# Six subtractions of a fold moved from VectorE to GpSimd, and five drains behind SyncE's last store

## The chip, the cores and the metric

The kernel runs on one core of a Trainium2 chip. The metric is device time in microseconds (us) of one execution; medians over several executions are quoted, lower is better. TensorE does the matrix products, VectorE and ScalarE the elementwise work, GpSimd small statistics and some DMA issues, SyncE most DMA issues. All runs told here were of the fast state.

## The reference, cut to what matters

```python
xn = layernorm(x)                                   # x: 1 x 2048 x 640, bf16
s  = irfft2(rfft2(xn) * (w_r + 1j * w_i))           # spectral filter
g  = silu((gelu(xn @ w_gate) * (xn @ w_up)) @ w_down)   # 640 -> 1536 -> 640
out = x + s * g
```

The 2048 rows lie in 16 slabs of 128. The forward transform of a pair of slabs starts with a *fold*: four sums and differences of a row with its own mirror image, which shorten the matrix product behind it.

## The kernel before

The kernel names its operations to a small planner (cut here). The planner holds an estimated cost for each and, when the kernel is built, puts all of them into one order for each engine; each engine's program is that list, with waits put in only where data or a buffer demands them. A changed cost or engine of one operation can therefore reorder every engine. The part that the change touches:

```python
    def fold(j, aps):                     # slabs 2j and 2j+1
        sxn, eo, xf, A = xn_of[j], Slot("ma"), Slot("mb"), Slot("mc")
        def f1(e):                        # L505: sum with the mirror image
            nc.vector.tensor_tensor(out=eo.tile[:, :, 0, :], in0=sxn.tile[:, :, 0:320], in1=sxn.tile[:, :, 639:319:-1], op=ALU.add)
        def f2(e):                        # L508: difference, the one that moves
            nc.vector.tensor_tensor(out=eo.tile[:, :, 1, :], in0=sxn.tile[:, :, 0:320], in1=sxn.tile[:, :, 639:319:-1],
                                    op=ALU.subtract)
        # f3 (L514, sum) and f4 (L519, difference) fold eo once more into xf   ... cut
        c = c_dve(640)
        t = add(f1, "DVE", c, (1, max(2 * j + 1, 3), 1), after=aps, new=[eo], use=[sxn])
        t = add(f2, "DVE", c, (1, max(2 * j + 1, 3), 1), after=[t], use=[sxn, eo])
        # ... f3, f4, then TensorE: L532 and L533 multiply xf by F1T
```

In the profile `s` is the normalised slab pair (written by L447, a subtract and multiply on VectorE), `ma` is `eo`, `mb` is `xf`. Around the folds VectorE also makes the gated products of the first half of the feed-forward part (L907) and the gate `G` (L990), which free or fill what TensorE's products L886 and L976 use.

The program ends with the planned order, and nothing behind it:

```python
        for t in plan.run():
            t.emit(t.on)
```

Of the kernel before, what the change touches and what calls it, by code (L numbers as in the profile page):

```python
# [13 lines left out]
ACT = mybir.ActivationFunctionType  # L14
# [100 lines left out]
class Plan:  # L115
# [12 lines left out]
    def add(self, emit, eng, cost, rank, after=(), new=(), use=(), size=0, slow=1.0, hold=0, order=(), lag=0, land=0):  # L128
        engs = eng if isinstance(eng, dict) else {eng: cost}
        t = Task(emit=emit, engs=engs, rank=rank, after=list(after), new=list(new), size=size, slow=slow, hold=hold, order=list(order), lag=lag, land=land,  # L130
                 seq=len(self.tasks))
        for s in (*new, *use):
            s.users.append(t)
        self.tasks.append(t)
        return t
# [23 lines left out]
    def run(self):  # L159
        left, now, order = list(self.tasks), 0.0, []  # L160
        while left:
            best, soon, held = None, None, {}
            for t in left:
                if t.hold:
                    for e in t.engs:
                        at = self.ready(t, e, now)
                        if at is not None and now < at <= now + t.hold:
                            held[e] = min(held.get(e, t.rank), t.rank)
            for t in left:
                for e in t.engs:  # L170
                    at = self.ready(t, e, now)
                    if at is None:
                        continue
                    at = max(at, self.free[e])
                    if at <= now and e in held and held[e] < t.rank:
                        at = now + 20
                    if at <= now and len(t.engs) > 1 and e == "DVE" and max(now, self.free["ACT"]) + t.engs["ACT"][0] <= now + t.engs[e][0] + self.PREFER:
                        at = max(now, self.free["ACT"]) + 20
                    if at <= now:
                        if best is None or (t.rank, t.seq) < (best[0].rank, best[0].seq):  # L180
                            best = (t, e)
                    elif soon is None or at < soon:
                        soon = at
            if best is None:
                if soon is None:
                    raise AssertionError("the plan is stuck at %d of %d" % (len(order), len(self.tasks)))
                now = soon
                continue
            t, e = best
            occ, lat = t.engs[e]  # L190
            t.on, t.start = e, now
            self.free[e] = now + occ
            if VERB: print(f"{now:9.0f} {occ:6.0f} {t.done or 0:9.0f} {e} {t.emit.__qualname__.split('kernel.<locals>.')[-1]} {t.rank}")
            t.done = now + lat
            if t.land:
                self.wire = max(self.wire, t.land - 3200)
                t.done = t.land
            elif t.size:
                self.wire = max(self.wire, now + occ + 900) + t.size * t.slow / 340.0
                t.done = self.wire + (1000 if now < 1000 else 2100 if now < 1700 else 2600 if now < 2700 else 3300 if now < 18000 else 2600 if now < 27000 else 1000) + t.lag  # L200
            for s in t.new:
                self.slots[s.tag].append(s)
            order.append(t)
            left.remove(t)
        return order


def c_pe(*ns):
    occ = sum(n / 2.4 + 2.5 for n in ns)
    return occ, occ + 240  # L210
# [6 lines left out]
def c_dve(n, rate=2, psum=False, extra=0):  # L217
    d = ((120 if psum else 58) + n / rate) / 0.96 + extra
    return d + 10, d + 130
# [3 lines left out]
def kernel(  # L223
# [11 lines left out]
    nc = tc.nc  # L235
# [50 lines left out]
    add = plan.add  # L286

    def place(slot, shape, dt=BF16):
        if slot.tag in ("sp", "pg", "pu"):
            slot.tile = psum.tile([P, *shape], dt, tag=slot.tag, name=slot.tag)  # L290
        else:
            slot.tile = work.tile([P, *shape], dt, tag=slot.tag, name=slot.tag, bufs=BUFS[slot.tag])
        return slot.tile
# [69 lines left out]
    def keep_warm(n, after, rank=(0, -9), ns=425):  # L363
        def go(e):
            if heat.tile is None:
                place(heat, (2, 512))
            for k in range(n):
                nc.tensor.matmul(heat.tile[:, k % 2, :], lhsT=idle.tile[:, 0:P], rhs=idle.tile,  # L368
                                 start=True, stop=True, skip_group_check=True)
        return add(go, "PE", (n * ns, n * ns), rank, after=after, new=[] if heat.users else [heat], use=[idle] + ([heat] if heat.users else []))  # L370
# [7 lines left out]
    t = add(blank, "DVE", (330, 400), (0, -9), new=[idle])  # L378
    t = warmed = keep_warm(6, [t])
# [120 lines left out]
    def fold(j, aps):  # L500
        sxn, eo, xf, A = xn_of[j], Slot("ma"), Slot("mb"), Slot("mc")

        def f1(e):
            place(eo, (2, 2, 320))
            nc.vector.tensor_tensor(out=eo.tile[:, :, 0, :], in0=sxn.tile[:, :, 0:320], in1=sxn.tile[:, :, 639:319:-1], op=ALU.add)  # L505

        def f2(e):
            nc.vector.tensor_tensor(out=eo.tile[:, :, 1, :], in0=sxn.tile[:, :, 0:320], in1=sxn.tile[:, :, 639:319:-1],  # L508
                                    op=ALU.subtract)

        def f3(e):
            place(xf, (2, 2, 2, 160))
            v = eo.tile.rearrange("p s e d -> p (s e) d")
            nc.vector.tensor_tensor(out=xf.tile[:, 0].rearrange("p s e d -> p (s e) d"), in0=v[:, :, 0:160],  # L514
                                    in1=v[:, :, 319:159:-1], op=ALU.add)

        def f4(e):
            v = eo.tile.rearrange("p s e d -> p (s e) d")
            nc.vector.tensor_tensor(out=xf.tile[:, 1].rearrange("p s e d -> p (s e) d"), in0=v[:, :, 0:160],  # L519
                                    in1=v[:, :, 319:159:-1], op=ALU.subtract)  # L520
        c = c_dve(640)
        t = add(f1, "DVE", c, (1, max(2 * j + 1, 3), 1), after=aps, new=[eo], use=[sxn])
        t = add(f2, "DVE", c, (1, max(2 * j + 1, 3), 1), after=[t], use=[sxn, eo])
        t = add(f3, "DVE", c, (1, max(2 * j + 1, 3), 1), after=[t], new=[xf], use=[eo])
        t = add(f4, "DVE", c, (1, max(2 * j + 1, 3), 1), after=[t], use=[xf, eo])
        outs = []
        for s in range(2):
            pa = Slot("sp")

            def mm(e, s=s, pa=pa):  # L530
                pt = place(pa, (2, 512))
                nc.tensor.matmul(pt[:, 0, :], lhsT=F1T, rhs=xf.tile[:, :, s, :, 0:128], start=True, stop=True)  # L532
                nc.tensor.matmul(pt[:, 1, 0:128], lhsT=F1T, rhs=xf.tile[:, :, s, :, 128:160], start=True, stop=True)  # L533

            def cp(e, s=s, pa=pa):
                if s == 0:
                    place(A, (2, D))
                copy_on(e, A.tile[:, s, :], flat(pa.tile)[:, 0:D])
            a = add(mm, "PE", c_pe(512, 128), (0, 20 + 2 * j + s), after=[t, tab_in["f1"]], new=[pa], use=[xf])
            outs.append(add(cp, either(640), None, (1, 2 * j + s), after=[a] + outs, new=[] if s else [A], use=[pa, A] if s else [pa]))  # L540
        stored[j] = dma(lambda: D2[:, 2 * j:2 * j + 2, :], lambda: A.tile, (0, -1, j), 327680, after=outs, use=[A], slow=1.1)

    lead = ("DVE", "ACT", "DVE", "ACT")
    for n1 in range(NSLAB):
        if n1 % 2 == 0:
            xn_of[n1 // 2] = Slot("s1")
# [18 lines left out]
    t = add(rows_pe, "PE", (215, 460), (0, 7), after=[*minused, turned[2]] + [roots[n1] for n1 in range(4)], new=[sr])  # L565
    t = add(lambda e: nc.vector.tensor_copy(out=RB[0:8, 0, 0, :], in_=sr.tile[0:8, 0, 0:P]), "DVE", c_dve(128, 1, True), (0, 3.5), after=[t], use=[sr])
# [30 lines left out]
    for ri, w in enumerate((A_w_r, A_w_i)):  # L597
        for G in range(8):
            b = 8 * G if G else 2
            turned_w[G].append(add(lambda e, ri=ri, w=w, G=G, b=b: nc.sync.dma_start(  # L600
                out=D4[:, b:8 * G + 8, ri, :], in_=bass.AP(tensor=w.tensor, offset=w.offset + (P - b) * L, ap=[[P * L, NSLAB], [-L, 8 * G + 8 - b], [1, LP]])),
                                   "SP", (650, 650), (2, G) if G < 2 else (3, G - 1.5), after=[turned[3]] if G < 2 else [B_in[3]], size=82432, slow=1.7))
        for a, n, b, first, width in ((0, 8, 0, 1088, LP), (8, 7, 0, 1152, LP), (15, 1, 0, 1024, LP), (0, 15, 1, P - 1, LP), (15, 1, 1, S - 1, L)):
            turned_w[0].append(add(lambda e, ri=ri, w=w, a=a, n=n, b=b, first=first, width=width: nc.gpsimd.dma_start(
                out=D4[a:a + n, b, ri, 0:width], in_=rows(w, first, n, width)), "POOL", (600, 600), (9, ri, b, a), after=[roots[15]], size=5152))
# [408 lines left out]
    with tc.manual_schedule():  # L1014
        for t in plan.run():
            t.emit(t.on)


# [28 lines left out]
```

## Time and profile before

| | before |
|---|---|
| time, median (3 runs, 202.13 to 202.86) | 202.7 us |
| profiled span | 200.7 us |
| TensorE without a pause | 24 us to its end at 196.74 us |
| end of TensorE's work to the end of the span | 4.0 us |

The prediction reads the page, its slices and the chain. Two more views of before are needed to compare with later. (In a line of a timeline stand the start and the length in us, engine, source line, operation, output<-inputs, shapes and the count.) First, from the groups by line: behind the count (x8) stand the busy time in us, the mean of one in ns, and the idle time of the engine in front of them. The first two steps of a fold cost 0.48 us each, all eight of each kind:

```profile
L508 DVE TENSOR_TENSOR ma<-s 128x640 bf16<-128x640 bf16 x8 | 3.9, 483 | 0.0
L505 DVE TENSOR_TENSOR ma<-s 128x640 bf16<-128x640 bf16 x8 | 3.8, 485 | 0.0
```

Second, the windows of 5 us where the last folds lie. After the width come the busy times of TensorE, its weight loads, VectorE, ScalarE and GpSimd with their instruction counts, then TensorE's granted clock, the DMA share and GB/s:

```profile
40.00:45.00 5.00, 5.00 (x39) 3.42 (x38) 4.56 (x13) 3.33 (x7) 4.83 (x10) 1.00 0.98 257
45.00:50.00 5.00, 5.00 (x39) 3.52 (x37) 3.19 (x10) 1.67 (x5) 3.48 (x7) 1.00 1.06 158
```

TensorE is full in both, and between 45 and 50 us VectorE has 1.8 us to spare. No VectorE instruction between 15 and 54 us is longer than 0.9 us.

### The profile page before, as it was taken

The page shows a single profiled execution, that of the slowest core. Times are in us where ns is not written, and L with a number is a line of the kernel's source. Part 1 is how long each engine was busy: PE and PEld are TensorE (multiplying, and loading weights), DVE is VectorE, ACT ScalarE, POOL GpSimd, SP SyncE. Part 2 cuts the span into 40 slices and gives each one's busy share as a digit, 9 for nine tenths or more (in the row PEclk, how much of TensorE's full clock was granted, in tenths as well). Part 3 has the DMA queues.
Part 4 walks back from the last instruction along what each step waited for, and adds up shares of the span by engine and source line. Part 5 has one row for each costly group of instructions (what it writes and reads, how often), then busy time and mean ns, then how long its engine had stood idle before and what let it go on. Part 6 is the DMA issues. An engine that isn't in the chain of part 4 may idle for free.

```text
span 200.7 us, 4126 instructions
## 1 busy us (share of the span) xinstructions
PE 195.5 (97%) x1527; PEld 118.2 (59%) x1527; DVE 148.6 (74%) x318; ACT 128.3 (64%) x226; POOL 32.8 (16%) x71
## 2 busy tenths in 40 slices
PE   7999999999999999999999999999999999999992
PEld 3994444667544655777755455467765555457781
DVE  3689999996524159999998999933157788787773
ACT  3899989763722767767775767233466565776451
POOL 2414333896000000000000000000004122211210
PEclk9999999999999999999999999999999999999999
DMA  6999999896639976333244110116704242332432
GB/s 180 325 316 325 339 393 225 207 257 171 207 76 349 340 179 135 92 97 122 61 118 132 68 65 1 69 64 215 309 3 141 90 134 98 102 104 92 131 103 67
DMA packets 35895, 32.63 MB, mean 163 GB/s; under 512 B 10910, under 2 KB 32930, under 8 KB 35874
## 3 DMA queue, kind: packets, MB, share of 16 engines
q1 hardware_dynamic: 34434, 29.49, 50.4%
q0 software_dynamic: 1152, 2.66, 4.9%
q10 hardware_dynamic: 288, 0.20, 0.5%
q8 instruction: 12, 0.20, 0.4%
q14 instruction: 9, 0.07, 0.1%
HBM read 22.51 MB, written 9.19 MB: 158 GB/s over the span
## 4 chain that ended last, share of the span: by engine, by line
PE 97%; DVE 0%; ACT 0%; issue 0%; DVEq 0%
PE pg L886 26%; PE pu L886 26%; PE pg L976 13%; PE pu L976 13%; PE sp L697 3%; PE sp L830 3%; PE sp L772 2%; PE sp L806 2%; PE sp L368 2%; PE sp L670 2%; PE sp L532 2%; PE sp L690 1%; PE sp L824 1%; PE sp L463 1%; PE sp L478 1%; PE sp L653 0%
## 5 line engine op out<-in xcount | busy, mean ns | idle before, releaser
L886 PE MATMUL pu<-xnT,Wu 128*128 128x512 bf16 (+1 forms) x245 | 57.6, 366 | 0.0
L886 PE MATMUL pg<-xnT,Wg 128*128 128x512 bf16 (+1 forms) x245 | 57.5, 366 | 0.0
L907 DVE TENSOR_TENSOR uT<-pu,ge 128x512 bf16<-128x512 f32 x46 | 31.8, 690 | 20.6 <-PE pu L886 17.5
L976 PEld LDWEIGHTS <-uT 128*128 128x128 bf16 x396 | 37.9, 98 | 13.5
L903 ACT ACTIVATE ge<-pg 128x512 bf16<-128x512 f32 x46 | 27.6, 599 | 24.9 <-PE pg L886 24.4
L886 PEld LDWEIGHTS <-Wg 128*128 128x128 bf16 x285 | 25.5, 99 | 22.1
L886 PEld LDWEIGHTS <-Wu 128*128 128x128 bf16 x285 | 25.0, 98 | 21.6
L976 PE MATMUL pg<-Wd,uT 128*128 128x320 bf16 (+2 forms) x204 | 30.8, 293 | 0.0
L296 ACT CAST ma<-sp 128x644 bf16<-128x644 f32 (+1 forms) x32 | 23.4, 792 | 9.7 <-PE sp L830 7.9
L976 PE MATMUL pu<-Wd,uT 128*128 128x320 bf16 (+1 forms) x192 | 29.3, 297 | 0.0
L932 POOL COPY xr<-s 1x1 bf16<-1x1 bf16 x1 | 0.2, 179 | 100.3 <-DVE s L856 100.3
L933 POOL DMA_DIRECT2D xr<-in_A_x_dram x16 | 8.8, 550 | 32.3 <-DVE res L960 30.2
L296 ACT CAST IU<-sp 128x640 bf16<-128x640 f32 x16 | 10.9, 691 | 4.2 <-PE sp L772 4.1
L296 ACT CAST Vt<-sp 128x640 bf16<-128x640 f32 x16 | 10.8, 691 | 3.7 <-PE sp L806 3.7
L296 ACT CAST mc<-sp 128x640 bf16<-128x640 f32 x16 | 10.8, 700 | 3.4 <-DMA D<-mc 2.8
L985 ACT ACTIVATE th<-pu 128x320 f32<-128x320 f32 x15 | 6.6, 438 | 9.6 <-PE pu L976 9.3
L990 DVE SCALAR_TENSOR_TENSOR G<-th,pg 128x320 bf16<-128x320 f32 x15 | 7.2, 483 | 7.1 <-ACT th L985 6.9
L985 ACT ACTIVATE th<-pg 128x320 f32<-128x320 f32 x15 | 6.7, 445 | 7.8 <-PE pg L976 7.7
L990 DVE SCALAR_TENSOR_TENSOR G<-th,pu 128x320 bf16<-128x320 f32 x15 | 7.3, 484 | 4.6 <-ACT th L985 4.4
L433 POOL TENSOR_TENSOR RSTD<-MVA,mh 128x1 f32<-128x1 f32 x12 | 9.8, 815 | 4.0 <-DVE MVA L415 3.2
L848 DVE TENSOR_TENSOR mb<-ma 128x640 bf16<-128x640 bf16 x8 | 3.9, 491 | 6.8 <-ACT ma L296 6.8
L960 DVE TENSOR_TENSOR res<-yg,xr 128x640 bf16<-128x640 bf16 (+2 forms) x18 | 8.0, 449 | 0.2
(107 smaller groups left out, 255.1 us busy)
## 6 DMA issues: line engine op xcount, KB each, us to landing
BU<-D SPq DMA_DIRECT2D x8, 640.0 KB
D<-mc SPq DMA_DIRECT2D x8, 320.0 KB
D<-IU SPq DMA_DIRECT2D x8, 320.0 KB
xr<-in_A_x_dram POOLq DMA_DIRECT2D x16, 160.0 KB, 2.6
out_dram<-res SPq DMA_DIRECT2D x15, 160.0 KB
Wg<-in_B_w_gate_dram SPq DMA_DIRECT2D x6, 320.0 KB
Wu<-in_B_w_up_dram SPq DMA_DIRECT2D x6, 320.0 KB
Wd<-in_B_w_down_dram SPq DMA_DIRECT2D x6, 320.0 KB
```

Source lines behind the costliest of these rows:

```text
L296: return nc.scalar.copy(out=out, in_=in_) if e == "ACT" else nc.vector.tensor_copy(out=out, in_=in_)
L433: nc.gpsimd.tensor_tensor(out=rstd, in0=var, in1=mh, op=ALU.pow)
L697: nc.tensor.matmul(into(q, ri), lhsT=sZ.tile[:, q, ri, :], rhs=FM[:, kinds[q][2] + (4 if ri and kind == 0 else 0), :], start=False, stop=T ...
L830: nc.tensor.matmul(into(q, s), lhsT=svs[s].tile[:, c, :], rhs=IM[:, q, :], start=False, stop=True, skip_group_check=True)
L886: nc.tensor.matmul(ps.tile[:, lo:hi + more], lhsT=w[:, c, t * P:(t + 1) * P], rhs=XR[:, c, lo + (lo > 0):hi + 1 if lo or more else hi] if ...
L903: nc.scalar.activation(out=ge.tile, in_=pg.tile if src is None else src, func=ACT.Gelu_apprx_tanh)
L907: nc.vector.tensor_tensor(out=u.tile, in0=pu.tile if src is None else src, in1=ge.tile, op=ALU.mult)
L933: nc.gpsimd.dma_start(out=sx.tile, in_=xv[:, n1, :])
L960: (nc.gpsimd if n1 in () else nc.vector).tensor_tensor(out=res.tile[:, lo:hi], in0=yg.tile[:, lo:hi], in1=sx.tile[:, lo:hi], op=ALU.add)
L976: nc.tensor.matmul(ps.tile[:, 0:hi - lo], lhsT=uT[grp, ks[i]].tile[:, j * P:(j + 1) * P], rhs=Wd[:, ks[i], lo:hi], start=(i == 0), stop=(i ...
L985: nc.scalar.activation(out=th.tile[:, 0:hi - lo], in_=ps.tile[:, 0:hi - lo], func=ACT.Tanh, scale=0.5)
L990: nc.vector.scalar_tensor_tensor(out=G2.tile[:, lo:hi], in0=th.tile[:, 0:hi - lo], scalar=1.0, in1=ps.tile[:, 0:hi - lo], op0=ALU.add, op1 ...
```

## The change

The intent is to relieve VectorE, which is 74% busy and nearly full while the folds run, by giving a part of its work to GpSimd, which is 16% busy. Six of the eight first differences (slabs 4 to 15) go to GpSimd; the planner is told 1.5 us for each. Five drains (instructions of SyncE that move no data; in the traces of the runs that have them each takes 7 to 137 ns) are put behind the last store that SyncE issues.

```diff
-                    if at <= now and len(t.engs) > 1 and e == "DVE" and max(now, ...
+                    if at <= now and "ACT" in t.engs and e == "DVE" and max(now, ...
...
         def f2(e):
-            nc.vector.tensor_tensor(out=eo.tile[:, :, 1, :], ...
+            (nc.gpsimd if e == "POOL" else nc.vector).tensor_tensor(out=eo.tile[:, :, 1, :], ...
...
-        t = add(f2, "DVE", c, (1, max(2 * j + 1, 3), 1), after=[t], use=[sxn, eo])
+        t = add(f2, *(("POOL", (1500, 1600)) if 2 <= j < 8 else ("DVE", c)), (1, max(2 * j + 1, 3), 1), after=[t], use=[sxn, eo])
...
         for t in plan.run():
             t.emit(t.on)
+        for _ in range(5):
+            nc.sync.drain(fusable=False)
```

A further line only changes quotation marks. The first hunk keeps an old rule from asking for a ScalarE cost where the choice is another engine.

More of the change, by code (lines that the diff above doesn't have):

```diff
@@ L176, in run @@
                         at = now + 20
-                    if at <= now and len(t.engs) > 1 and e == "DVE" and max(now, self.free["ACT"]) + t.engs["ACT"][0] <= now + t.engs[e][0] + self.PREFER:
+                    if at <= now and "ACT" in t.engs and e == "DVE" and max(now, self.free["ACT"]) + t.engs["ACT"][0] <= now + t.engs[e][0] + self.PREFER:
                         at = max(now, self.free["ACT"]) + 20
@@ L507, in f2 @@
         def f2(e):
-            nc.vector.tensor_tensor(out=eo.tile[:, :, 1, :], in0=sxn.tile[:, :, 0:320], in1=sxn.tile[:, :, 639:319:-1],
+            (nc.gpsimd if e == "POOL" else nc.vector).tensor_tensor(out=eo.tile[:, :, 1, :], in0=sxn.tile[:, :, 0:320], in1=sxn.tile[:, :, 639:319:-1],
                                     op=ALU.subtract)
@@ L541, in fold @@
         stored[j] = dma(lambda: D2[:, 2 * j:2 * j + 2, :], lambda: A.tile, (0, -1, j), 327680, after=outs, use=[A], slow=1.1)
-    lead = ("DVE", "ACT", "DVE", "ACT")
+    lead = ('DVE', 'ACT', 'DVE', 'ACT')
     for n1 in range(NSLAB):
```

## The prediction

> **What bounds the kernel now.** I read the page first: busy time by engine, the slices, and the chain that ended last.
>
> ```profile
> PE 195.5 (97%) x1527; PEld 118.2 (59%) x1527; DVE 148.6 (74%) x318; ACT 128.3 (64%) x226; POOL 32.8 (16%) x71
> PE   7999999999999999999999999999999999999992
> DVE  3689999996524159999998999933157788787773
> PE 97%; DVE 0%; ACT 0%; issue 0%; DVEq 0%
> ```
>
> The first line is busy time, the next two are the span in 40 slices, the last is the chain by engine. TensorE works from slice 2 to slice 39, and the chain is TensorE almost throughout. In the windows of 10 us TensorE is busy 10.00 of 10.00 everywhere from 10 to 180 us. I also added the matmuls up in their order with the spacing that the trace shows (five of 512 columns every 1.08 us, twelve of 320 columns every 1.63 us): the starts keep this spacing, so there are no hidden pauses. Outside that stretch, 4 us pass at each end. So VectorE's time is worth nothing by itself; it matters only where VectorE makes TensorE wait.
>
> How close is VectorE to doing that? The timeline of 16 to 52 us, where the folds lie, engine by engine:
>
> ```profile
> 20.97 0.44 DVE L447 TENSOR_SCALAR s<-X,NM,RSTD 128x640 bf16<-128x640 bf16 x1
> 21.32 0.48 DVE L508 TENSOR_TENSOR ma<-s 128x640 bf16<-128x640 bf16 x1
> ...
> 27.86 0.48 DVE L519 TENSOR_TENSOR mb<-ma 128x640 bf16<-128x640 bf16 x1
> ...
> 37.89 0.69 DVE L907 TENSOR_TENSOR uT<-R,ge 128x512 bf16<-128x512 f32 x1
> ...
> 39.25 0.50 DVE L519 TENSOR_TENSOR mb<-ma 128x640 bf16<-128x640 bf16 x1
> ```
>
> ```profile
> 30.22 0.38 PE L532 MATMUL sp<-mb,F1T 128*128 128x512 bf16 x1
> ...
> 39.42 0.98 PE L976 MATMUL pg<-Wd,uT 128*128 128x320 bf16 x6
> ...
> 41.05 0.38 PE L532 MATMUL sp<-mb,F1T 128*128 128x512 bf16 x1
> ```
>
> L508 is the subtraction that moves, L519 ends a fold, L532 is TensorE's use of that fold. The fold of slabs 6 and 7 is ready at 28.3 and used at 30.2; that of slabs 8 and 9 is ready at 39.8 and used at 41.05. The last gated product (L907) ends at 38.6, and the down projection that needs it starts at 39.42. So the margins are 0.8 to 1.9 us, while VectorE is busy 10.00 of 10.00 us from 30 to 40.
>
> **What the Trainium skill says.**
> - "GPSIMD Engine Reference", section 3.1: about 2.6 cycles an element for a two-input elementwise instruction at 1.2 GHz, and 4497 ns measured at 2048 elements. 640 x 2.6 / 1.2 = 1387 ns, with some 60 ns fixed: an estimate of 1.45 us for one moved subtraction. The trace of before has no wide GpSimd instruction to test this.
> - "VectorE: DVE Perf Modes", the perf-mode tier table: tensor_tensor in bf16 from SBUF runs at two elements a cycle. The trace agrees: 0.48 us each for 640 elements, starting every 0.40 us.
> - "SBUF — State Buffer", section Who interferes with whom: a VectorE instruction with two SBUF inputs contends with a GpSimd instruction that reads SBUF, and the loser waits for the whole instruction. The trace hints at it. The same 128x1 power (L433) on GpSimd:
>
> ```profile
> 27.33 0.55 POOL L433 TENSOR_TENSOR RSTD<-MVA,mh 128x1 f32<-128x1 f32 x1
> ...
> 35.84 1.94 POOL L433 TENSOR_TENSOR RSTD<-MVA,mh 128x1 f32<-128x1 f32 x1
> ...
> 39.12 1.44 POOL L433 TENSOR_TENSOR RSTD<-MVA,mh 128x1 f32<-128x1 f32 x1
> ```
>
> It takes 0.55 us beside PSUM work and 1.44 to 1.94 us where VectorE runs two-SBUF-input instructions back to back.
> - "VectorE: DVE Perf Modes", The DRAIN you can't avoid: drains of the launch code are about 12 ns. The trace's records of SyncE's drains are 7 and 13 ns, and one of 114 ns in the closing barrier.
>
> **The change part by part.**
> 1. Removed from VectorE: six L508, 6 x 0.40 = 2.4 us between 21 and 51 us.
> 2. Added to GpSimd: six of about 1.45 us, 8.7 us. GpSimd was busy 3.3, 5.7 and 8.3 us in the three windows of 10 us from 20 to 50, so it has room.
> 3. Moved: the scheduler reorders all engines. TensorE's list holds the same matmuls, so its work is unchanged. With the spacing above, the use of the fold of slabs 6 and 7 moves from 30.22 to 38.88 us, those of slabs 8 to 13 keep their places or move by under 1 us, that of slabs 14 and 15 comes 1.9 us earlier, and the first matmul on the regrouped data comes 1.1 us earlier, at 64.3. Its data has room: in before the regrouping loads stood behind the filter loads (issued 58.7); now they stand in front, and I estimate the first 640 KB there by 59 (at the 366 GB/s of 61 to 67 us).
> 4. The lock. I walk VectorE's new list with durations of before and GpSimd's 1.45 us. First subtraction (slabs 4, 5): beside it stand a statistics and a PSUM product, nothing lost. Second: it wins the pair at about 26.0 and holds a normalisation (L447) until 27.5; VectorE is 0.9 us behind. Third: about 29.6 to 31.1, in front of eight instructions with two SBUF inputs; VectorE is about 2.4 us behind, less about 0.5 (three subtractions gone, 1.2, against 0.75 of statistics brought forward). The fold of slabs 6 and 7 then ends at 39.6 to 40.0 against 38.88 wanted: TensorE waits 0.7 to 1.1 us. The late products also hold the two pu buffers, which is the same wait, not another: I count 1.1 us.
> 5. The other three stand close together between about 42 and 48 us, with GpSimd's small DMA issues in between. They can hold the two closing steps of the folds, up to 1.3 us; I count half, 0.6 us.
> 6. The drains: SyncE's last store is issued by 197.95, the last store of all lands at about 199.35, and SyncE waits for it anyway. Five drains of some 60 ns from start to start fit into the 1.4 us. 0.0 us; shifting SyncE's instruction addresses could move the close by up to 0.4 us either way (the trace has a gap of 0.39 us between SyncE's last drains), no direction chosen.
>
> Sum: 1.1 + 0.6 + 0.0 = 1.7 us, all of it pauses in TensorE. 202.7 + 1.7 = 204.4; as some waits may fall into margins I take 204.2.
>
> ```profile
> 195.91 0.83 PE L976 MATMUL pg<-Wd,uT 128*128 128x128 bf16 x12
> ...
> 197.75 0.35 ACTq L965 DMA_DIRECT2D out_dram<-res  x1
> ```
>
> These show the close: last matmuls, then the last store, from ScalarE. None of it depends on the folds.
>
> **The rivals.**
> - *All hidden.* If the lock costs VectorE no more than the 2.4 us that it saves, TensorE never waits and the time stays at 202.5 to 202.9. For: margins of 0.8 to 1.9 us and a schedule drawn up with 1.5 us for each subtraction. Against: that schedule has no lock in it.
> - *GpSimd becomes the bound of the folds.* If a subtraction takes 2.5 us or more beside VectorE, as the 0.55 grown to 1.94 suggests, each closing half of a fold waits on VectorE's in-order queue and blocks the gated products behind it: 3 to 5 us, 206 to 208. For: the stretched powers. Against: those tiny instructions may have waited for their turn only once.
> - *A gain.* A shorter VectorE list would have to fill TensorE pauses, and there are none: at best the 0.4 us of the close, 202.3.
>
> **Range and chances.** Low end: everything hidden, 202.6. High end: 2.5 us subtractions with most of their wait exposed, 206.6. Two per cent is 4.05 us: slower needs over 206.75, at the edge of the second rival, 0.11; faster needs under 198.6, which TensorE's 195.5 us of work plus the two ends rules out, 0.01; within, 0.88.
>
> **What would show it.** Right: TensorE's busy time still near 195.5 but gaps of 1 to 2 us in all between 35 and 50 us, released by VectorE (L519 or L907); L508 on GpSimd at 1.4 to 1.6 us alone and more beside VectorE; some VectorE instructions of 0.4 to 0.5 us stretched to over 1 us; nothing new after 65 us but the shift; the close unchanged. Wrong: TensorE still without gaps (first rival), L508 over 2.5 us (second), new waits in the filter stage from 70 to 130 us, where VectorE is again over 90% busy and which I assume has the same margins as before, or a close that changes by more than 0.4 us.

## The result, and the profile after

The changed kernel took **205.31 us** (median of 4 runs, 205.13 to 206.53) beside 202.57 (4 runs, 202.13 to 202.86). The ratio is 1.015 with a 95% interval of 1.0106 to 1.0194. A ratio here is always the mean time of one kernel's fast runs over the mean of the other's of the same rounds, so it is not quite the ratio of the medians. The change is slower by 1.5%, which counts as the same at the 2% line.

The profiled span grew by 2.8 us, from 200.7 to 203.5 us. First the page again: busy time, TensorE's and VectorE's slices, and the chain.

```profile
PE 194.7 (96%) x1508; PEld 117.3 (58%) x1527; DVE 152.0 (75%) x312; ACT 128.3 (63%) x226; POOL 41.2 (20%) x77
PE   7999999986999999999999999999999999999993
DVE  3789999999423239999998989942246789777764
PE 91%; DVE 4%; DMA 2%; issue 1%; SPq 0%; ACT 0%; DVEq 0%
```

The first line holds the surprise. VectorE executes six instructions fewer (312 for 318) and is busy 3.4 us *more* (152.0 for 148.6). TensorE's slices show a dip (8, 6) in slices 9 and 10 of 5.1 us each, and VectorE has 4% of the chain, where it had 0. (Nineteen of TensorE's records are missing in this trace; its list of matmuls is the same.)

The windows of the dip, in the columns of above:

```profile
40.00:45.00 5.00, 4.46 (x34) 2.99 (x33) 5.00 (x9) 2.97 (x6) 4.98 (x6) 1.00 0.69 172
45.00:50.00 5.00, 3.09 (x23) 1.94 (x22) 5.00 (x8) 2.11 (x5) 4.98 (x7) 1.00 0.72 177
```

In the second window VectorE is busy 5.00 us with only 8 instructions, where it did 10 in 3.19 us before. So it isn't given more to do; each takes longer. TensorE does 3.09 of 5.00 us. Its timeline shows the pauses, each with its length and what ended it in square brackets:

```profile
38.80 0.39 PE L532 MATMUL sp<-mb,F1T 128*128 128x512 bf16 x1
...
43.87 1.79 PE L976 MATMUL pg<-Wd,uT 128*128 128x320 bf16 x12 [0.54 <-DVE G L990]
47.56 0.39 PE L532 MATMUL sp<-mb,F1T 128*128 128x512 bf16 x1 [1.91 <-DVE mb L519]
...
51.09 0.39 PE L532 MATMUL sp<-mb,F1T 128*128 128x512 bf16 x1 [0.36 <-DVE mb L519]
```

These three pauses are 0.54 + 1.91 + 0.36 = 2.81 us. (A fourth gap, 0.15 us at 183 us, is a missing record: e2, the same kernel without drains and with all 1527 records, has five matmuls there where this trace has four, and no gap.) TensorE's last matmul ends 3.26 us later than before (200.00 for 196.74). The rest lies in how the records overlap: five matmuls of 512 columns are recorded as 1.24 us but start every 1.08, so a pause costs about 0.16 us more than its recorded length, and 2.81 + 3 x 0.16 = 3.29. The first of the four lines is the fold that I had feared for: it starts at 38.80 without any wait.

What VectorE did there, and GpSimd beside it:

```profile
43.74 1.37 DVE L505 TENSOR_TENSOR ma<-s 128x640 bf16<-128x640 bf16 x1
45.03 0.47 DVE L990 SCALAR_TENSOR_TENSOR G<-th,pu 128x320 bf16<-128x320 f32 x1
45.43 0.48 DVE L514 TENSOR_TENSOR mb<-ma 128x640 bf16<-128x640 bf16 x1
45.83 1.68 DVE L519 TENSOR_TENSOR mb<-ma 128x640 bf16<-128x640 bf16 x1
47.43 0.47 DVE L990 SCALAR_TENSOR_TENSOR G<-th,pg 128x320 bf16<-128x320 f32 x1
47.83 1.60 DVE L505 TENSOR_TENSOR ma<-s 128x640 bf16<-128x640 bf16 x1
```

```profile
43.15 1.52 POOL L508 TENSOR_TENSOR ma<-s 128x640 bf16<-128x640 bf16 x1
...
45.69 1.47 POOL L508 TENSOR_TENSOR ma<-s 128x640 bf16<-128x640 bf16 x1
...
47.66 1.41 POOL L508 TENSOR_TENSOR ma<-s 128x640 bf16<-128x640 bf16 x1
```

Each stretched VectorE instruction shown here begins while a GpSimd subtraction runs and ends just behind it: GpSimd's second ends at 45.69 + 1.47 = 47.16, VectorE's L519 at 47.51. L990, which reads one operand from PSUM, stays at 0.47. The groups by line say the same in sum: six L508 now stand under GpSimd, and the mean of L505, which did not change, went from 485 to 819 ns.

```profile
L508 POOL TENSOR_TENSOR ma<-s 128x640 bf16<-128x640 bf16 x6 | 9.0, 1499 | 0.7 <-DVE s L447 0.7
L505 DVE TENSOR_TENSOR ma<-s 128x640 bf16<-128x640 bf16 x8 | 6.5, 819 | 0.0
```

Seven VectorE instructions between 15 and 54 us are longer than 0.9 us: four L505 or L514 (1.15, 1.08, 1.37, 1.60), two L447 (1.52 each) and one L519 (1.68). Over their usual 0.44 to 0.48 us they take 6.6 us more; the six moved instructions took 2.9 us of recorded length away (2.4 us of VectorE's time, since neighbours overlap by 0.08 us).

The close is *shorter* than before. From the issue of SyncE's last store to its last record it is 2.60 us, where it was 3.05. So the span's 2.8 us are 3.26 us of later TensorE less 0.45 us of shorter close.

### The profile page after: what moved, and what is told of

Its sections match the earlier page's. It is cut to its first block, busy times and chain, and to the rows that moved or that the text cites. A ratio compares the mean times of both kernels' runs of the same rounds, so it can differ in the third digit from the quotient of the medians.

```text
span 203.5 us, 4112 instructions
## 1 busy us (share of the span) xinstructions
PE 194.7 (96%) x1508; PEld 117.3 (58%) x1527; DVE 152.0 (75%) x312; ACT 128.3 (63%) x226; POOL 41.2 (20%) x77
## 4 chain that ended last, share of the span: by engine, by line
PE 91%; DVE 4%; DMA 2%; issue 1%; SPq 0%; ACT 0%; DVEq 0%
PE pu L886 25%; PE pg L886 25%; PE pu L976 12%; PE pg L976 12%; PE sp L697 3%; PE sp L830 3%; PE sp L772 2%; PE sp L806 2%; DMA X<-in_A_x_dram 2%; PE sp L670 2%; PE sp L532 2%; DVE ma L505 1%; PE sp L824 1%; DVE mb L519 1%; PE sp L690 1%
## 5 line engine op out<-in xcount | busy, mean ns | idle before, releaser
L886 PE MATMUL pu<-xnT,Wu 128*128 128x512 bf16 (+1 forms) x239 | 57.3, 366 | 0.4
L886 PE MATMUL pg<-xnT,Wg 128*128 128x512 bf16 (+1 forms) x232 | 55.8, 365 | 0.5
L886 PEld LDWEIGHTS <-Wg 128*128 128x128 bf16 x285 | 25.2, 98 | 22.3
L886 PEld LDWEIGHTS <-Wu 128*128 128x128 bf16 x285 | 25.1, 98 | 21.6
L976 PE MATMUL pu<-Wd,uT 128*128 128x320 bf16 (+1 forms) x192 | 30.0, 297 | 0.0
L990 DVE SCALAR_TENSOR_TENSOR G<-th,pg 128x320 bf16<-128x320 f32 x15 | 7.3, 484 | 7.7 <-ACT th L985 7.4
L990 DVE SCALAR_TENSOR_TENSOR G<-th,pu 128x320 bf16<-128x320 f32 x15 | 7.2, 483 | 5.6 <-ACT th L985 5.5
L296 ACT CAST Z<-sp 128x1024 bf16<-128x1024 f32 x8 | 7.9, 1014 | 2.4 <-PE sp L670 2.4
L433 POOL TENSOR_TENSOR RSTD<-MVA,mh 128x1 f32<-128x1 f32 x12 | 8.9, 748 | 1.0 <-DVE MVA L415 0.2
L508 POOL TENSOR_TENSOR ma<-s 128x640 bf16<-128x640 bf16 x6 | 9.0, 1499 | 0.7 <-DVE s L447 0.7
```

The source lines that it names most:

```text
L296: return nc.scalar.copy(out=out, in_=in_) if e == "ACT" else nc.vector.tensor_copy(out=out, in_=in_)
L433: nc.gpsimd.tensor_tensor(out=rstd, in0=var, in1=mh, op=ALU.pow)
L508: (nc.gpsimd if e == "POOL" else nc.vector).tensor_tensor(out=eo.tile[:, :, 1, :], in0=sxn.tile[:, :, 0:320], in1=sxn.tile[:, :, 639:319:- ...
L886: nc.tensor.matmul(ps.tile[:, lo:hi + more], lhsT=w[:, c, t * P:(t + 1) * P], rhs=XR[:, c, lo + (lo > 0):hi + 1 if lo or more else hi] if ...
L976: nc.tensor.matmul(ps.tile[:, 0:hi - lo], lhsT=uT[grp, ks[i]].tile[:, j * P:(j + 1) * P], rhs=Wd[:, ks[i], lo:hi], start=(i == 0), stop=(i ...
L990: nc.vector.scalar_tensor_tensor(out=G2.tile[:, lo:hi], in0=th.tile[:, 0:hi - lo], scalar=1.0, in1=ps.tile[:, 0:hi - lo], op0=ALU.add, op1 ...
```

## The experiments

The theory: a GpSimd instruction that reads SBUF shuts VectorE out of its instructions with two SBUF inputs (and of L447) for its whole length; the late three subtractions do it where TensorE has no margin; the drains shorten the close. The rivals: the planner's new order is what costs; a subtraction of 1.5 us where 0.48 stood is a longer chain, lock or no lock; the drains cost, or do nothing.

| run | median us (range, runs) | before on the same chip | ratio, 95% interval |
|---|---|---|---|
| e1_drains_only | 202.11 (201.82 to 202.61, 6) | 202.76 | 0.9975, 0.9962 to 0.9989 |
| e2_no_drains | 205.97 (205.81 to 206.12, 4) | 202.76 | 1.0163, 1.015 to 1.0176 |
| e3_memset | 203.04 (202.04 to 203.67, 6) | 202.76 | 1.0016, 0.9995 to 1.0037 |
| e7_lock_only | 207.01 (206.05 to 208.03, 6) | 202.76 | 1.0214, 1.0185 to 1.0243 |
| e4_memset_twice | 202.32 (201.99 to 202.51, 4) | 202.56 | 0.9975, 0.9934 to 1.0016 |
| e5_first3 | 202.83 (202.56 to 203.62, 4) | 202.56 | 1.0008, 0.9963 to 1.0053 |
| e6_last3 | 206.80 (205.35 to 206.92, 4) | 202.56 | 1.0175, 1.0114 to 1.0237 |
| e8_planned | 207.55 (206.71 to 207.92, 4) | 202.56 | 1.0228, 1.0182 to 1.0275 |
| e9_drains2 | 202.26 (202.05 to 202.93, 6) | 202.75 | 0.9984, 0.9968 to 1.0 |
| e10_drains5 | 201.99 (201.87 to 202.28, 5) | 202.75 | 0.9966, 0.9953 to 0.9978 |

### The two parts apart: e1_drains_only and e2_no_drains

e1 is the kernel before with the drains alone; e2 is the changed kernel without them.

```diff
 # e1, on the kernel before                  # e2, on the changed kernel
+        for _ in range(5):                  -        for _ in range(5):
+            nc.sync.drain(fusable=False)    -            nc.sync.drain(fusable=False)
```

> The kernel before with the five drains alone, nothing else moved. Theory of the close: in the trace of before SyncE pauses 0.39 us ten instructions after its last store, behind its last wait; in the changed kernel the same pause stands ten instructions after the last store too, but in front of the wait for the landing, and costs nothing. So the span falls by 0.3 to 0.5 us, to about 200.3 (time about 202.2), with TensorE as before. Rival: the drains are idle filler and the shorter close of the changed kernel comes from its other instruction counts: span 200.7, time 202.6.

> The changed kernel without its drains. Theory of the close: slower than the changed kernel by the exposed pause, 205.6 to 205.8 us against 205.3, TensorE's waits unchanged (3 to 3.5 us between 38 and 52 us). Rival: 205.3.

The drains alone gain 0.65 us (202.11 for 202.76); the subtractions without drains cost 3.21 us (205.97 for 202.76), with pauses of 0.55, 1.90 and 0.36 us in TensorE as in the changed kernel. (e2 is 0.2 us above the range that I had written down, and its pauses, 2.81 us, lie just under the 3 to 3.5.) So the change is two effects of opposite sign, and its loss is all from the move. e1 beats both kernels, though by less than 2%.

### Order, length or lock: e3_memset, e4_memset_twice and e7_lock_only

e3 keeps the changed kernel's order on every engine, but GpSimd fills the half tile with zeros where it subtracted, so it writes SBUF and reads nothing. Its result is wrong on purpose (relative error 0.024). e4 fills it twice, so that GpSimd is busy almost as long as with the subtraction; wrong on purpose too. e7 is the reverse: the kernel before, its order kept, with six extra GpSimd subtractions on a scratch tile that nobody waits for.

```diff
 # e3 and e4, on the changed kernel, where e == "POOL"
-            nc.gpsimd.tensor_tensor(out=eo.tile[:, :, 1, :], ..., op=ALU.subtract)
+            nc.gpsimd.memset(eo.tile[:, :, 1, :], 0.0)          # e4: twice, 1.0 and 0.0
 # e7, on the kernel before, behind VectorE's own L508
+            if 2 <= j < 8:
+                nc.gpsimd.tensor_tensor(out=XR[:, :, 0:128], in0=XR[:, :, 256:384], in1=XR[:, :, 511:383:-1], op=ALU.subtract)
```

> The changed kernel with every engine's order untouched, but GpSimd fills the half with zeros (a memset, which reads nothing) in place of the subtraction; the result is wrong on purpose. Lock theory (a GpSimd instruction that reads SBUF shuts out VectorE's instructions with two SBUF inputs): the stretched VectorE instructions go back to under 0.8 us, TensorE has no waits over 0.3 us after 25 us, time 202.0 to 202.6. Order theory (the schedule itself places TensorE's steps too early): TensorE still waits over 1.5 us between 38 and 52 us, time 204 or more. It cannot tell the lock from a merely slow GpSimd; the next run does.

> As the run with the memset, but with two memsets one behind the other in place of each subtraction: GpSimd is busy 2 x 0.63 = 1.26 us, nearly as long as with the subtraction, and still reads nothing; wrong on purpose. If it is GpSimd's reading that shuts VectorE out: no VectorE instruction over 0.8 us, time within 0.5 us of the run with one memset, 202.5 to 203.6. If GpSimd's occupation or lateness is what costs (folds waiting for it, or any GpSimd write shutting VectorE out): stretched or idle VectorE between 40 and 50 us and 204 to 205.5.

> The kernel before with every engine's order untouched and all subtractions on VectorE, plus six idle subtractions of 640 elements on GpSimd (on a tile no longer in use) that nothing waits for, at the same places of GpSimd's order. Lock theory: VectorE instructions beside them stretch to over 1 us (about 6 us in all, none of it paid back by saved work), TensorE waits 2 to 5 us between 25 and 55 us, time 204.5 to 207.5. Order theory and slow-GpSimd theory: nobody waits for these instructions, so the time stays at 202.4 to 202.9.

With the fill the loss is gone: 203.04 and 202.32 us, and in e3 no VectorE instruction is over 0.84 us. e3's GpSimd and TensorE timelines:

```profile
42.50 0.65 POOL L508 MEMSET ma<- 128x640 bf16 x1
```

```profile
50.34 0.38 PE L532 MATMUL sp<-mb,F1T 128*128 128x512 bf16 x1 [0.50 <-ACT mc L296]
```

The expectation of e3 that no wait over 0.3 us would be left was missed: there is one of 0.50 us, ended by ScalarE, which itself waited for an earlier store to leave a buffer. VectorE has no part in it. So the new order costs something of its own, between nothing (e4, with one pause of 0.38 us, is as quick as the drains alone) and 0.9 us (e3 against e1); the runs scatter too much to say more.

e4 answers the rival of length. GpSimd's two fills take 1.26 to 1.32 us together, near the subtraction's 1.4 to 1.7, with the same instructions behind them, and VectorE's fold steps beside them keep their 0.48 to 0.49 us. Length alone does not do it. L447, which has one tensor input, is another matter. VectorE's and GpSimd's timelines of e4:

```profile
28.17 0.48 DVE L514 TENSOR_TENSOR mb<-ma 128x640 bf16<-128x640 bf16 x1
28.57 0.94 DVE L447 TENSOR_SCALAR s<-X,NM,RSTD 128x640 bf16<-128x640 bf16 x1
```

```profile
28.01 1.31 POOL L508 MEMSET ma<- 128x640 bf16 x2
```

The fold step passes, and L447 ends 0.18 us behind the second fill. In e3 and e4, of seven L447 that begin while a fill is recorded, six take 0.52 to 0.94 us and end 0.18 us behind a fill (the seventh begins in the fill's last 0.07 us); behind the recorded subtractions that hold them L447 end 0.18 to 0.20 us as well. So fills hold L447 too, only for a shorter time. (e4's expectation, no VectorE instruction over 0.8 us and 202.5 to 203.6 us, was missed by both numbers.)

e7 answers the rest. Nothing waits for its subtractions and the order is the one of before, yet it is slower than e2, which has no drains either and ran in the same rounds (207.01 for 205.97 us). VectorE's, GpSimd's and TensorE's timelines:

```profile
42.09 2.28 DVE L516 TENSOR_TENSOR mb<-ma 128x640 bf16<-128x640 bf16 x1
44.29 0.47 DVE L992 SCALAR_TENSOR_TENSOR G<-th,pu 128x320 bf16<-128x320 f32 x1
```

```profile
42.68 1.32 POOL L511 TENSOR_TENSOR XR<-XR 128x640 bf16<-128x640 bf16 x1
```

```profile
45.22 0.39 PE L534 MATMUL sp<-mb,F1T 128*128 128x512 bf16 x1 [1.26 <-DVE mb L521]
51.23 0.39 PE L534 MATMUL sp<-mb,F1T 128*128 128x512 bf16 x1 [2.03 <-DVE mb L521]
```

(Line numbers are two higher than in the other kernels.) A fold step of VectorE grows from 0.48 to 2.28 us and ends just behind GpSimd's idle subtraction, and TensorE pauses behind the fold. (GpSimd's other work comes later too, but VectorE is busy 4.97 of 5.00 us from 45 to 50 us: it is held, and does not wait for that work.) The effect on the fold steps needs only the reads of GpSimd. That is the theory shown, for its core: beside a reading GpSimd instruction VectorE's two-input SBUF instructions can be held to its end; beside a writing one they aren't. It goes the other way as well: e7's third subtraction, from 36.43 us, took 2.46 us for 1.32, while VectorE's L508 in the middle of it took its usual 0.48.

One detail stays open. This L516 *begins* 0.6 us before GpSimd's record does. The changed kernel's L447 at 41.90 us is held 1.52 us, to 43.42, though the recorded subtraction runs from 43.15 to 44.67; in e8 an L447 at 40.85 us takes 1.54 us and is through at 42.39, before the subtraction recorded at 42.50; e7's L521 at 49.57 us, 1.60 us long and in front of its second pause, lies between two recorded subtractions (to 49.30, from 51.43). It matters: the changed kernel's first pause, 0.54 us, comes behind that L447. In these times GpSimd's records show mainly DMA issues, so these are a rival holder. Against it, no VectorE instruction of the kernel before is over 0.76 us between 15 and 54 us, beside such issues or not; and in e3 and e4, with the issues kept and a fill behind them, the L447 at this place takes 0.83 and 0.85 us. So the length goes with what stands behind the issues. It may be that some part of GpSimd already works on the next instruction in its list before the record begins; I have argued that, not shown it.

### Which subtractions: e5_first3 and e6_last3

```diff
-  if 2 <= j < 8 else
+  if 2 <= j < 5 else      # e5: slabs 4 to 9
+  if 5 <= j < 8 else      # e6: slabs 10 to 15
```

> The changed kernel with only the subtractions of slabs 4 to 9 (the first three) on GpSimd, drains kept; its order is nearly that of the changed kernel. From the trace of the changed kernel, where TensorE waits under 0.3 us before 42 us although three VectorE instructions there are stretched: TensorE waits at most 1 us, time 202.1 to 203.2. My prediction on record put the larger share (1.1 of 1.7 us) on the second and third subtraction: then 203.2 or more.

> Only the subtractions of slabs 10 to 15 (the last three) on GpSimd, drains kept; its order is nearly that of the kernel before up to 40 us. From the trace of the changed kernel: these three carry nearly all of the loss, four VectorE instructions stretched to 1.4 to 1.7 us, TensorE waits 2 to 3.5 us between 42 and 54 us, time 204 to 205.8. If the loss came from the first three carrying VectorE late into this stretch: under 203.

e5 has three stretched VectorE instructions (0.97, 1.60, 1.08 us) and no pause of TensorE at all; 202.83 us. e6 has two (L447 2.06, L514 2.75 us) and one pause of 3.18 us. The loss is the late three's. The early ones hold VectorE too, for 2.2 us over the usual lengths in e5, but VectorE regains it before TensorE asks. (e5 is still 0.7 us above e1 of another round. Its trace puts 0.5 us of that before the first subtraction at 20.31 us: TensorE's clock becomes full at 7.25 us, in before at 6.31, and the first L886 of 512 columns starts at 15.07 us, in before at 14.56. The rest may be the new order or scatter.)

e6 took longer than the 204 to 205.8 us expected, and its TensorE timeline says why:

```profile
47.89 0.39 PE L532 MATMUL sp<-mb,F1T 128*128 128x512 bf16 x1 [3.18 <-DVE mb L519]
...
48.45 3.37 PE L976 MATMUL pu<-Wd,uT 128*128 128x320 bf16 x12
```

and so does the window of 4 us behind the pause (clock in the column of 0.57):

```profile
48.00:52.00 4.00, 4.00 (x18) 2.26 (x18) 3.31 (x10) 1.77 (x4) 3.37 (x6) 0.57 0.35 81
```

Twelve matmuls that elsewhere take 1.79 us take 3.37. The trace's clock record is exact: from 48.48 us on, 3.41 us at half clock. The Trainium skill, "TensorE: Matmul & The Clock Gate", section What's actually happening, tells of it: the clock is halved after about 3.4 us of idling, judged in fixed windows of 3413 ns. The length agrees to the digit; the condition is milder here. I laid windows of 3413 ns back from the change of the clock, and counted TensorE's busy share in the one in front: 17% in e6, and 41% in e7, which has the same 3.41 us at half clock behind a pause of only 2.03 us. On the same grid the poorest window of the changed kernel is 50% busy and that of e2 52%, and neither was slowed.

Half clock for 3.41 us loses 1.71 us. With it the ledgers close to about 0.2 us: e6, 3.18 + 1.71 = 4.89 for a TensorE end 4.73 us later than before; e7, 1.26 + 2.03 + 1.71 = 5.00 for 5.08. (Left out are the 0.16 us that each pause costs besides, and an earlier full clock at the start, at 4.10 and 4.52 us for 6.31; they partly cancel.) The timed runs of e6 fit it: three at a mean clock of 0.991 to 0.992 took 206.79 to 206.92, the one at 1.0 took 205.35. (Those of e7 sort less cleanly: 207.63 us came at 0.997.) All four runs of the changed kernel had 0.996 to 1.0, so its loss is not of this kind. The windows don't move with the kernel, so where a pause falls in them is luck; a worse draw would cost it 1.7 us.

### Telling the planner: e8_planned

If the stretching is regular, one might tell the planner of it. e8 is the changed kernel with 1.1 us added to the planned cost of L505 in the six folds.

```diff
-  t = add(f1, "DVE", c, ...
+  t = add(f1, "DVE", (c[0] + 1100, c[1] + 1100) if 2 <= j < 8 else c, ...
```

> The changed kernel, with the scheduler told that the first addition of each of these six folds takes 1.1 us longer, which is about what VectorE loses to each subtraction in the trace (6.6 us over six). It moves other matmuls in front of the folds. If the loss is lock time that the schedule did not know of: TensorE waits under 1 us from 25 to 60 us. The folds end some 6 us later, so the regrouped data and the filter stage come later; if that has room, 202.0 to 203.0; if it has none, new waits after 60 us and 203 to 206. The rival that the lock cannot be scheduled around expects 204.5 to 206 with the waits where they were.

TensorE has no pause and ends at 196.66 us, as in before; but the time is the worst of all, 207.55 us. TensorE's slices and VectorE's timeline at the end:

```profile
PE   7999999999999999999999999999999999999930
```

```profile
197.03 0.49 DVE L848 TENSOR_TENSOR mb<-ma 128x640 bf16<-128x640 bf16 x1 [1.72 <-ACT ma L296]
...
201.55 0.63 DVE L960 TENSOR_TENSOR res<-yg,xr 128x256 bf16<-128x256 bf16 x3 [0.22 <-DMA out_dram<-res]
```

The planner, believing VectorE slower, moved the folds back: the last is used at 60.5 us, where it was 51.9 before. The stages behind it come later, and the feed-forward matmuls that don't depend on them fill TensorE meanwhile; but the last slabs' way through VectorE (L848 to L960) then lies behind TensorE's end instead of beside it, from 197.0 to 202.2 us. The loss has not been avoided, only moved to the tail; that the later folds are what moved it I read from the order, and no run tests it. Of the two outcomes that I had written down neither came about as told; later waits were the nearer one, and the time is above its range.

### The drains: e9_drains2 and e10_drains5

In the traces of before and of e1, SyncE stands still for about 0.4 us after its tenth instruction behind the last store, whichever instruction that is. e9 tests this with two drains; e10 is e1 again as the standard on the same chip.

```diff
 # on the kernel before; e10 has range(5)
+        for _ in range(2):
+            nc.sync.drain(fusable=False)
```

> The kernel before with two drains behind SyncE's last store instead of five. Theory of the fixed place: in the trace of before and in that of five drains alone SyncE pauses 0.39 us after its tenth instruction behind the last store, whatever those instructions are. With two drains the tenth is the wait for the landing of SyncE's own last store (1.59 us after the issue in before), so the pause falls behind it and stays exposed from about 1.6 to 2.0 us; the close is shorter than before's by at most 0.1 us, the ratio to before 0.999 to 1.001. Rival, that any drains behind the last store shorten the close (by emptying something early): the same 0.4 to 0.65 us as five drains, ratio 0.997 to 0.998, and no pause behind the landing.

> The kernel of e1_drains_only once more, as the standard for the run with two drains on the same chip: both theories expect 0.4 to 0.65 us less than before, ratio 0.9968 to 0.998, with SyncE's pause in front of the wait for the landing.

From SyncE's records, in us behind the issue of its last store (before: at 197.61 us):

| | before | two drains (e9) | five drains (e10) | changed kernel |
|---|---|---|---|---|
| starts of the tenth and eleventh instruction | 1.83, 2.24 | 1.59, 2.00 | 1.07, 1.48 | 1.07, 1.48 |
| wait for the landing of its own last store recorded | 1.59 | 1.59 | 1.63 | 1.63 |
| wait for ScalarE's last store recorded | 1.76 | 2.00 | 1.75 | 1.76 |
| last record | 3.05 | 2.88 | 2.58 | 2.60 |

Instructions there that wait for nothing mostly start every 0.05 to 0.09 us. The standstill of 0.40 to 0.41 us follows the tenth instruction in all four, as the theory of the fixed place has it. The other traces say what the place is fixed to: e5 and e8, whose SyncE has one record more in front of its last store, stand still behind the ninth. In all twelve traces it is the 207th record of SyncE's list. Without drains it comes when both stores have landed and everybody waits for SyncE. With five it comes before the landing, which SyncE would have waited for anyway, and costs nothing. With two it falls between the two landings and is hidden for a small part: the close is 0.17 us shorter than before's, a little more than the 0.1 that I had allowed. So the drains don't do anything by draining; they are padding that moves a standstill. The times agree less sharply: the ratio of two drains, 0.9984, misses the 0.999 to 1.001 written down and lies between the two theories, and its interval reaches up to 1.0. The verdict rests on the records. (e10 came out 0.1 us faster than its range.) What the standstill is, no trace shows: it has no record of its own. Two things speak for the fetching of instructions, which is argued only: its place in the list is fixed, and in every trace an instruction fetch of 8 KB (DMA queue 14) starts 1.0 to 1.3 us behind that 207th record.

## Why the prediction was right or wrong

The time, 205.31 us for a predicted 204.2, lies inside the range. The sum was 1.7 us of TensorE's pauses and nothing at the close; it came out as 3.26 us of later TensorE and 0.45 us less at the close. Point by point:

- **The bound, and that VectorE's relief is worth nothing: right.** TensorE had no pause to fill, so removing 2.4 us from VectorE could gain nothing, and in e3, where VectorE is relieved without the lock, nothing is gained beyond the drains.
- **GpSimd's subtraction at 1.45 us: right.** Measured mean 1.499 us, between 1.40 and 1.70.
- **The lock: right, as a mechanism.** The Trainium skill's rule ("SBUF — State Buffer", Who interferes with whom) for VectorE instructions with two SBUF inputs is shown by e7 against e3 and e4, and the trace of after has the stretched instructions of over 1 us that I asked for.
- **Step 4, second and third subtraction, 1.1 us: wrong in size, 0.0 measured.** The fold of slabs 6 and 7 started at 38.80 us without a wait; VectorE's step before it ended at 38.75. Both subtractions did hold VectorE (L447 for 1.52 us, L514 for 1.08), which is 1.7 us over their usual, where I had allowed 2.4 after the third. My walk also placed the third at 29.6, behind the fold's sum; on the chip it waits only for the normalisation and ran at 27.89, beside that sum and a PSUM product. The planner's "after" is an order of issue, not a wait across engines. e5 confirms that the early ones cost TensorE no pause.
- **Step 5, the last three, 0.6 us: wrong in size, 2.8 measured.** This is the largest miss. I counted half of two closing steps. In the trace each of the three holds a two-input instruction, and a normalisation just ahead of them is held too: 1.08 + 0.88 + 1.20 + 1.12 = 4.3 us of stretch within 8 us. VectorE had 1.8 us to spare in the window of 45 to 50 us and its margins to the folds were 0.8 to 1.9 us, so most of it came through. e6, these three alone, has 3.18 us of pause.
- **Step 6, the drains, 0.0 with up to 0.4 either way: a gain of 0.45, just outside.** A close that changes by more than 0.4 us was one of my signs of being wrong, and it came true. 0.45 us at the close, 0.65 and 0.76 us in the medians of e1 and e10. I had looked at the gap between SyncE's last drains and called it movable; I had not counted instructions to see where five more would push it.
- **Nothing new after 65 us: right. Gaps of 1 to 2 us in all: too low**, 2.81 us, though released by VectorE as told.
- **The rivals.** "All hidden" fell by e2. "GpSimd becomes the bound" is right in its shape (gated products and folds held by VectorE's in-order queue, 3 us) and wrong in its cause: GpSimd's subtractions stayed under 1.71 us; in the changed kernel VectorE was the one that waited.

So the mechanism was right, and that the time came out near was luck in part, by three errors that partly cancelled: step 4 was 1.1 us too high, step 5 2.2 us too low (together 2.81 us of pauses for 1.7), the close 0.45 us too long.

What stays open: the early hold at 41.9 us, ahead of the recorded subtraction; and what SyncE's standstill is. The best version found is the kernel before with the five drains alone, 202.11 and 201.99 us in its two runs.

## What to carry to other kernels

An idle GpSimd is not free help for a VectorE that works from SBUF: each reading GpSimd instruction can hold a two-input VectorE instruction for its whole 1.4 to 1.7 us, so moving 0.40 us of work cost VectorE 1.1 us on average (6.6 us over six). Before you move work, list what the other engine will be executing beside it and how much margin the consumer of *that* has; holds of the same kind were free at 28 us and cost 2.8 us at 45. And pauses of TensorE are to be kept short in sum, since a window with too many of them is followed by 3.4 us at half clock.

## What the Trainium skill lacked or had wrong

- "TensorE: Matmul & The Clock Gate", What's actually happening: its table of the two states asks for an idle window of about 3.4 us before the clock is halved. Here a pause of 2.03 us was enough where the window of 3413 ns in front was 41% busy; windows of 50% and 52% were not followed by it.
- "SBUF — State Buffer", Who interferes with whom: it says that whole instructions block; that in a trace VectorE can be held before GpSimd's instruction is recorded is not in that section. Here L516 was held from 42.09 us, with a subtraction recorded from 42.68, and L447 from 41.90 to 43.42 us, with one recorded from 43.15.
- The same section has the 2-port modes contend with GpSimd in general, without a number for fills. If L447 runs in such a mode (no run shows its mode), the runs agree: beside GpSimd's fills of 0.63 to 0.69 us six of them took 0.52 to 0.94 us for 0.44 and ended 0.18 us behind a fill.
- "VectorE: DVE Perf Modes", The DRAIN you can't avoid: about 12 ns for a drain of the launch code, and nothing on drains that a kernel asks for. Those on SyncE showed 134 to 137 ns for the first and 7 ns for each further one, 0.05 us from start to start.
- No page has it: SyncE stands still for 0.40 to 0.41 us behind the 207th record of its list near the end, in all twelve traces, with zero, two and five drains.
